# Attention and two feed-forward stages on one core: key scores in eight small matmuls, gate-weight splits ahead of the activation's, a new operand order, an earlier load

## The chip, the cores and the metric

The kernel runs on one core of a Trainium2 chip. The metric is the device time of one execution in microseconds (us), from the first to the last instruction with what lies around it. All arithmetic is in 32-bit floats. On TensorE most operands are split into a high part (type fp32r) and a low part, and three matmuls (high by high, low by high, high by low) stand for one.

## The reference, cut to what matters

```
sm_attn(qq, kk, vv): softmax(qq kk^T / sqrt(64)) vv        # 8 batches, 8 heads, 576 positions, head size 64
p_packed = sm_attn(p, k, v)                                # p: 32 rows for each head
out = sm_attn(q, p_packed, p_packed)
x = rows of out, 4608 x 512
xn = x / rms(x) * rms_g
y = (silu(xn @ w_gate) * (xn @ w_val)) @ w_out             # 512 -> 1536 -> 512
h = y @ w_in ; g = max(h, 0) + alpha * min(h, 0)
result = g @ w_out2                                        # 512 -> 2048 -> 512
```

## The kernel before

The order of the instructions on every engine is the order in which the program issues them; a scheduler does not move them. Each engine works through its own list in order and waits at an instruction whose operands, or whose output buffer, are not ready.

The program has an opening, a first phase of 12 chunks (`CH`, `c` = 0 to 11) of 512 or 320 token columns, and a second phase over five pairs of token blocks for the last feed-forward stage. The change touches the opening and the first phase.

In the first phase a chunk runs over 12 steps (`f`, blocks of 128 of the 1536 hidden units). A step makes a gate tile and a value tile in PSUM (`blk_in`, the second tensors `ps_g`, `ps_v`), takes Tanh on ACT, multiplies on DVE, splits the result into `hh` (ACT) and `hl` (DVE) in `hsplit`, and one step later `blk_out` multiplies them by the output weights into four accumulators `ps_y`. The operands of `blk_in` are the normalized attention weights `xh`, `xl` of the chunk's tokens and, instead of values and gate weights apart, their product: `wg_job(b, j)` multiplies the packed values of batch `b` by the `j`-th part of the gate and value weights (`ps_wg`, L685) and splits it into `wgh` (ACT) and `wgl` (DVE). `JOBS` says in which steps these jobs run.

Between these matmuls stands the attention of later batches and chunks. `k_steps` (one for each batch) attends from `p` to the keys and values, `q_steps` from the queries to the packed result. Both are generators, and `work` and `burst` advance them a little at fixed places of a step: `burst` those pieces that give TensorE work, `work` the vector pieces. In `k_steps`, S1 transposes `p`, S2 transposes the keys of a group of four heads, S3 makes their scores, EX the exponentials, S4 transposes these and S5 multiplies by the values.

The tiles `ps_g`, `ps_v`, `ps_at` and `ps_wg` take turns in four PSUM banks (`bank`), so that a new gate tile must wait until one of the tiles before it has been read. `conv` (opening and chunk 0) and `late` (`conv_late`, from chunk 1) convert weights that arrive as 64-bit words; `next(late)` runs in odd steps at the third call of `work`, and in every step of a 512-column chunk.

All DMAs are issued by SP, in program order.

In the kernel before, `pbd` holds `p` with the rows of two heads on the diagonal of a 64-row tile and zeros beside them, and a key tile holds, for each partition, the same row of the four heads side by side. So the scores are full matmuls over two heads at once:

```
nc.tensor.transpose(t[...], kv_t[b, "k", g][:, r, 2 * c:2 * c + 2, :], ident[0:KP, 0:KP])
nc.tensor.matmul(out=t[c * 64:(c + 1) * 64, 0:w], lhsT=pT[:, 2 * g + c, :],
                 rhs=kT[g][:, c * S + hf * w:c * S + (hf + 1) * w], start=True, stop=True)
```

Of the kernel before, what the change touches and what calls it, by code (L numbers as in the profile page):

```python
# [8 lines left out]
F32 = mybir.dt.float32  # L9
# [9 lines left out]
def attention_moe_moe2_kernel(ctx, tc, q, k, v, p, w_gate, w_val, w_out, rms_g, w_in2, w_out2, alpha, out):  # L19
    nc = tc.nc  # L20
# [105 lines left out]
    with tc.manual_schedule():  # L126
# [18 lines left out]
        def load_p(b):  # L145
            for e in range(2):
                for g in range(G):
                    nc.sync.dma_start(
                        out=pbd[(e ^ g) * NP:(e ^ g) * NP + NP, 2 * g:2 * g + 2, e * D:(e + 1) * D],
                        in_=p[b].rearrange("(g c e) n d -> e g n c d", g=G, e=2)[e, g],  # L150
                    )
# [6 lines left out]
        def load_kv():  # L158
            if not kv_list:
                return  # L160
            if late_kv[0] is not None and kv_list[-1][0]:
                late_kv[0] += 1
                return
            b, nm, g = kv_list.pop()
            t = ap.tile([KP, HG * KR, D], F32, tag="kv", name=nm + "t", bufs=3)
            src = (k if nm == "k" else v)[b, g * HG:(g + 1) * HG].rearrange("h (p r) d -> p h r d", r=KR)
            if nm == "k":
                t = t.rearrange("p (r h) d -> p r h d", r=KR)
                for h in range(HG):
                    nc.sync.dma_start(out=t[:, :, h], in_=src[:, h])  # L170
            else:
                t = t.rearrange("p (h r) d -> p h r d", r=KR)
                nc.sync.dma_start(out=t, in_=src)
            kv_t[b, nm, g] = t
# [189 lines left out]
        def k_steps(b, bk):  # L364
            par = b % 2
            yield 2
            pT = ap.tile([128, H // 2, 64], F32, tag="pT", name="pT")
# [3 lines left out]
            def S1():  # L371
                t = bk()
                for c in range(4):
                    nc.tensor.transpose(t[:, c * 64:(c + 1) * 64], pbd[:, c, :], ident[0:64, 0:64])
                return lambda: evac(pT, t[:, 0:256].rearrange("p (c x) -> p c x", c=4), True)

            def S2(g, n):
                t = bk()
                if n == 0:
                    kT[g] = ap.tile([128, 2 * S], F32, tag="kT", name="kT")  # L380
                for m in range(4):
                    c, r = divmod(4 * n + m, KR)
                    nc.tensor.transpose(
                        t[:, m * KP:(m + 1) * KP], kv_t[b, "k", g][:, r, 2 * c:2 * c + 2, :], ident[0:KP, 0:KP]
                    )
                return lambda: evac(kT[g][:, n * 384:(n + 1) * 384], t[:, 0:384], n % 2 == 0 or b < 2)

            def S3(g):
                w = S // 2
                for hf in range(2):  # L390
                    t = bk()
                    for c in range(2):
                        nc.tensor.matmul(
                            out=t[c * 64:(c + 1) * 64, 0:w],
                            lhsT=pT[:, 2 * g + c, :],
                            rhs=kT[g][:, c * S + hf * w:c * S + (hf + 1) * w],
                            start=True, stop=True,
                        )
                    s1[g, hf] = t
# [9 lines left out]
            def EX(g):  # L409
                w = S // 2  # L410
                E1[g] = ap.tile([128, S], F32, tag="E1", name="E1")
                for hf in range(2):
                    nc.scalar.activation(
                        out=E1[g][:, hf * w:(hf + 1) * w], in_=s1.pop((g, hf))[:, 0:w], func=ACTF.Exp,
                        bias=st[g][:, 2:3], scale=scale, accum_out=st[g][:, 3 + hf:4 + hf],
                    )
# [332 lines left out]
        qa.run()  # L749
        conv(2)  # L750
        warmup(3)
        qb.run()
        conv(2)
        qb.run()
        warmup(3)
        conv(2)
        qa.run()
        conv(2)
        warmup(3)
        qa.run()  # L760
        qb.run(2)
        conv_to(4)
        wg_job(0, 0)
        xh, xl = new_x()
        for ids, o in of_chunk[0]:
            x_split(ids, xh, xl, o)
# [118 lines left out]
        for c, (t0, n, cuts) in enumerate(CH):  # L885
# [72 lines left out]
            def blk_in(f, off, tag):  # L958
                t = bank(tag)[:, 0:n]
                j, o = f // 2, off + f % 2 * 128  # L960
                for lo, hi, b in cuts:
                    for g in range(G):
                        wh, wl = wgt[b, j, g]
                        mm3(
                            t[:, lo:hi], wh[:, o:o + 128], wl[:, o:o + 128],
                            xh[:, g, lo:hi], xl[:, g, lo:hi], g == 0, g == G - 1,
                        )
# [8 lines left out]
            for f in range(NF):  # L976
# [33 lines left out]
                nc.vector.tensor_tensor(out=s, in0=s, in1=tv, op=ALU.mult)  # L1010
                hs[f] = hsplit(s, n)
# [263 lines left out]
```

## Time and profile before

| | |
|---|---|
| Median of 3 runs | 1677.42 us (1677.4 to 1677.53) |
| Profiled execution | 1677.25 us, span 1675.5 us |
| Mean granted TensorE clock | 0.989 |
| TensorE (PE) busy | 1605.1 us, 96% |
| VectorE (DVE) busy | 1124.2 us, 67% |
| ScalarE (ACT) busy | 708.8 us, 42% |
| GpSimd (POOL) busy | 278.7 us, 17% |

A share of busy time is a mean over stages with different limits. What counts for this change is where TensorE stands idle, what it then waits for, and how long the pieces take that are replaced. One fp32 matmul leaves two records, so that "x8" can be four matmuls.

### The profile page before, as it was taken

The numbers are of one execution on the slowest core, as the hardware profiler recorded it, in microseconds if no ns is written. First come the engines' busy times: TensorE is split into PE (matmuls) and PEld (weight loads), VectorE is DVE, ScalarE is ACT, GpSimd is POOL, SyncE is SP. The second block draws the span as 40 slices with busy tenths as digits, with TensorE's granted clock in tenths as the row PEclk, the third lists the DMA queues.
The fourth block names the chain that finished last, engine by engine and source line by source line (L and its number), as shares of the span: only waits on it lengthen the run. The fifth ranks groups of instructions, "written<-read, shape, count | busy, mean of one in ns | idle before, by whom it ended". The sixth has DMA issues, their size and how long they took to land.

```text
span 1675.5 us, 28072 instructions
## 1 busy us (share of the span) xinstructions
PE 1605.1 (96%) x10378; PEld 1341.9 (80%) x10378; DVE 1124.2 (67%) x2109; ACT 708.8 (42%) x1533; POOL 278.7 (17%) x262
## 2 busy tenths in 40 slices
PE   6799899999999999999999999999999999999998
PEld 4466787888878878888888788888888888987997
DVE  4786557666566665665547888677757775776775
ACT  3566445555455454555445333421341133224224
POOL 1442123233233311001002662000000000000000
PEclk9699999999999999999999999999999999999999
DMA  9876546635565465663334665734464455657553
GB/s 223 274 238 190 171 125 184 174 83 178 161 187 165 131 208 169 209 195 117 115 101 156 232 232 193 266 138 170 157 232 150 158 174 203 217 198 264 189 183 126
DMA packets 234472, 303.07 MB, mean 181 GB/s; under 512 B 95200, under 2 KB 113632, under 8 KB 234336
## 3 DMA queue, kind: packets, MB, share of 16 engines
q1 hardware_dynamic: 234336, 301.28, 56.0%
q8 instruction: 82, 1.34, 0.3%
q14 instruction: 54, 0.44, 0.1%
HBM read 245.64 MB, written 55.57 MB: 180 GB/s over the span
## 4 chain that ended last, share of the span: by engine, by line
PE 44%; DVE 5%; DMA 2%; ACT 2%; issue 2%; POOL 1%; SPq 0%; DVEq 0%; ACTq 0%; POOLq 0%
PE ps_g L122 7%; PE ps_g L123 7%; PE ps_g L124 7%; PE ps_y L123 7%; PE ps_y L122 7%; PE ps_y L124 7%; DVE hl L113 1%; DMA in_l<-os_dram 1%; DVE in_l L113 1%; POOL i_raw L863 1%; ACT hh L110 1%; DMA i_raw<-w_dram 1%; DMA in_l<-lo_dram 1%; DVE tl L1073 1%; PE ps_v L123 1%
## 5 line engine op out<-in xcount | busy, mean ns | idle before, releaser
L122 PE MATMUL ps_y<-hh,in_h 128*128 128x320 f32 (+1 forms) x576 | 207.1, 360 | 3.5 <-ACT hh L110 3.5
L110 ACT ACTIVATE hh<-tl 128x512 fp32r<-128x512 f32 (+1 forms) x80 | 47.1, 588 | 375.2 <-DVE tl L1080 375.2
L124 PE MATMUL ps_y<-hh,in_l 128*128 128x320 f32 (+1 forms) x576 | 195.2, 339 | 2.6 <-DMA in_l<-lo_dram 2.6
L123 PE MATMUL ps_y<-hl,in_h 128*128 128x320 f32 (+1 forms) x576 | 195.6, 340 | 0.6
L1006 DVE SCALAR_TENSOR_TENSOR s<-s,ps_g 128x320 f32<-128x320 f32 (+1 forms) x132 | 71.3, 540 | 143.2 <-ACT s L1001 143.0
L110 ACT ACTIVATE hh<-s 128x320 fp32r<-128x320 f32 (+1 forms) x144 | 75.6, 525 | 213.3 <-DVE s L1010 213.3
L122 PEld LDWEIGHTS ps_y<-hh,in_h 128*128 128x128 f32 x576 | 109.1, 189 | 56.5 <-issue 43.0
L113 DVE TENSOR_TENSOR hl<-s,hh 128x320 fp32r<-128x320 f32 (+1 forms) x144 | 85.2, 592 | 85.1 <-ACT hh L110 85.1
L122 PE MATMUL ps_g<-xh,wgh 128*128 128x256 f32 (+3 forms) x384 | 123.3, 321 | 12.7 <-DVE wgl L113 4.9
L320 POOL TENSOR_TENSOR in_l<-w_raw,in_h 128x512 fp32r<-128x512 f32 x72 | 93.8, 1302 | 216.6 <-ACT in_h L110 176.0
L122 PE MATMUL ps_g<-yh,w 128*128 128x512 f32 (+1 forms) x336 | 125.3, 373 | 3.9 <-ACT th L1181 3.8
L123 PE MATMUL ps_g<-yl,w 128*128 128x512 f32 (+1 forms) x336 | 124.8, 371 | 0.0
L124 PE MATMUL ps_g<-yh,w 128*128 128x512 f32 (+1 forms) x336 | 124.8, 371 | 0.0
L123 PE MATMUL ps_g<-xl,wgh 128*128 128x256 f32 (+3 forms) x384 | 117.0, 305 | 4.5 <-DVE xl L113 4.5
L124 PEld LDWEIGHTS ps_y<-hh,in_l 128*128 128x128 f32 x576 | 109.1, 189 | 11.7 <-DMA in_l<-lo_dram 3.4
L122 PE MATMUL ps_v<-xh,wgh 128*128 128x256 f32 (+3 forms) x384 | 116.8, 304 | 0.2
L124 PE MATMUL ps_g<-xh,wgl 128*128 128x256 f32 (+3 forms) x384 | 116.3, 303 | 0.0
L123 PEld LDWEIGHTS ps_y<-hl,in_h 128*128 128x128 f32 x576 | 109.5, 190 | 8.3 <-DVE hl L113 1.9
L123 PE MATMUL ps_v<-xl,wgh 128*128 128x256 f32 (+3 forms) x384 | 116.1, 302 | 0.0
L124 PE MATMUL ps_v<-xh,wgl 128*128 128x256 f32 (+3 forms) x384 | 115.9, 302 | 0.0
L122 PE MATMUL ps_y<-in_h,hh 128*128 128x512 f32 x288 | 112.4, 390 | 1.6 <-DMA in_h<-os_dram 0.9
L123 PE MATMUL ps_y<-in_l,hh 128*128 128x512 f32 x288 | 113.2, 393 | 0.7 <-DVE in_l L113 0.2
(184 smaller groups left out, 4002.8 us busy)
## 6 DMA issues: line engine op xcount, KB each, us to landing
w<-w_dram SPq DMA_DIRECT2D x224, 256.0 KB, 5.1
gv_raw<-gv_dram SPq DMA_DIRECT2D x168, 256.0 KB, 3.7
o_raw<-w_dram SPq DMA_DIRECT2D x52, 512.0 KB, 4.1
w_dram<-w SPq DMA_DIRECT2D x88, 256.0 KB, 2.2
in_l<-lo_dram SPq DMA_DIRECT2D x59, 256.0 KB, 4.2
w<-in_moe_w_out_dram SPq DMA_DIRECT2D x28, 512.0 KB, 4.0
kt<-in_k_dram SPq DMA_DIRECT2D x64, 144.0 KB, 3.5
vt<-in_v_dram SPq DMA_DIRECT2D x16, 576.0 KB, 5.5
```

Source lines behind the costliest of these rows:

```text
L110: nc.scalar.activation(out=hi, in_=src, func=ACTF.Copy)
L113: nc.vector.tensor_tensor(out=lo, in0=src, in1=hi.bitcast(F32), op=ALU.subtract)
L122: nc.tensor.matmul(out=o, lhsT=lh, rhs=rh, start=first, stop=False, skip_group_check=more)
L123: nc.tensor.matmul(out=o, lhsT=lh, rhs=rl, start=False, stop=False, skip_group_check=more)
L124: nc.tensor.matmul(out=o, lhsT=ll, rhs=rh, start=False, stop=last, skip_group_check=more)
L320: nc.gpsimd.tensor_tensor(out=l, in0=raw[u], in1=h.bitcast(F32), op=ALU.subtract)
L863: nc.gpsimd.tensor_tensor(out=out, in0=x, in1=y, op=op)
L1006: nc.vector.scalar_tensor_tensor(out=s, in0=s, scalar=1.0, in1=tg, op0=ALU.add, op1=ALU.mult)
L1073: nc.vector.tensor_tensor(out=out, in0=x, in1=y, op=ALU.add)
```

## The change

It has five parts.

1. **Keys by row pairs.** `p` is loaded twice, once into each half of the head dimension's 128 columns (`pd`, two DMAs in place of four, and no zeros to write first). A key tile now lies head by head in the order of DRAM, so that a group is loaded in one DMA (two for batch 0) in place of four, in runs of 1,536 bytes in place of 256. S2 transposes two neighbouring rows of one head at a time: even rows land on partitions 0 to 63, odd rows on 64 to 127. S3 makes the scores in eight matmuls of 64 rows by 32 columns, each at its own place in the array (`tile_position`), even rows into one bank and odd rows into the other. EX writes the two banks interleaved.
2. **Combined gate weights split ahead of the activation.** From chunk 1 on the job of a step is issued right after the product, ahead of `hsplit` and of the second call of `work`, and no longer in `burst`.
3. **The operand's low part last in a chunk's first tile.** In step 0 of each chunk the six matmuls of a cut take `xh` four times and then `xl` twice.
4. **Late weights loaded a step ahead.** The first `next(late)` only issues loads.
5. **A new order of the opening**, in which the two query chains and the conversions alternate in smaller pieces, and each `x_split` follows its own chain.

```
-        pbd = ap.tile([64, H // 2, 128], F32, name="pbd")
+        pd = ap.tile([128, G, 2, D], F32, name="pd")
...
-        nc.vector.memset(pbd, 0.0)
...
+            src = p[b].rearrange("(g h) n d -> (h n) g d", g=G)
             for e in range(2):
...
+                nc.sync.dma_start(out=pd[:, :, e, :], in_=src)
...
-            if nm == "k":
-                t = t.rearrange("p (r h) d -> p r h d", r=KR)
-                for h in range(HG):
-                    nc.sync.dma_start(out=t[:, :, h], in_=src[:, h])
...
+            t = t.rearrange("p (h r) d -> p h r d", r=KR)
+            n_h = 2 if nm == "k" and b == 0 else HG
+            for h in range(0, HG, n_h):
+                nc.sync.dma_start(out=t[:, h:h + n_h], in_=src[:, h:h + n_h])
...
         def conv_late():
             ahead = [load_wide(u, one, NST) for u in units2[:2]]
+            yield
...
+                for e in range(2):
+                    s1[g, e] = bk()
+                for h in range(HG):
+                    for e in range(2):
+                        rows = slice(e * D, (e + 1) * D)
                         nc.tensor.matmul(
...
+                            out=s1[g, e][(h ^ g) * NP:(h ^ g) * NP + NP, 0:w],
+                            lhsT=pT[rows, g, h * NP:(h + 1) * NP],
+                            rhs=kT[g][rows, h * w:(h + 1) * w],
                             start=True, stop=True,
+                            tile_position=(e * D, (h ^ g) * NP),
                         )
...
-                for jb in jobs:
+                for jb in jobs if c == 0 else ():
                     wg_job(*jb)
...
+                for lo, hi, b in cuts if f == 0 else []:
+                    steps = [(xh, w, g) for w in range(2) for g in range(G)]
+                    steps += [(xl, 0, g) for g in range(G)]
...
                 nc.vector.tensor_tensor(out=s, in0=s, in1=tv, op=ALU.mult)
+                for jb in JOBS[c].get(f, ()) if c else ():
+                    wg_job(*jb)
                 hs[f] = hsplit(s, n)
                 work(f, 2)
```

On TensorE the order outside the opening and outside step 0 of a chunk stays; what stands in it changes. In step 1 of chunk 0, after a gate-weight job, the scores of a key group (`kT`, `pT`) stood ahead of `blk_out` like this before:

```order
L685 MATMUL ps_wg<-gv_raw,ppG 32x512 x8
L393 MATMUL ps_at<-kT,pT 64x288 x4
L122 MATMUL ps_y_567<-hh,in_h 128x512
L123 MATMUL ps_y_567<-hl,in_h 128x512
L124 MATMUL ps_y_567<-hh,in_l 128x512
```

and stand like this now:

```order
L683 MATMUL ps_wg<-gv_raw,ppG 32x512 x8
L390 MATMUL ps_at<-kT,pT 32x288 x8
L122 MATMUL ps_y_558<-hh,in_h 128x512
L123 MATMUL ps_y_558<-hl,in_h 128x512
L124 MATMUL ps_y_558<-hh,in_l 128x512
```

Four matmuls that give 64 rows of scores have become eight that give 32, at the same place. There are 16 such groups in the program, two of them in the opening and three in chunk 0.

On DVE, in steps 1 and 2 of chunk 1, the first late conversion (its weights are `w_1896`, its result `w_1900`) stood right behind the splits of step 1, and the query chain's transposes out of PSUM (`A_1925<-ps_at`) behind it:

```order
L1006 SCALAR_TENSOR_TENSOR s<-s,ps_g 128x320
L1010 TENSOR_TENSOR s<-s,ps_v 128x320
L113 TENSOR_TENSOR hl<-s,hh 128x320
L113 TENSOR_TENSOR wgl<-ps_wg,wgh 128x512 x2
L232 TENSOR_SCALAR w_1900<-w_1896 128x512
L578 STREAM_TRANSPOSE A_1925<-ps_at 128x256 x2
L580 TENSOR_REDUCE s_1770<-A_1925 128x16
```

Now the same steps read:

```order
L1023 SCALAR_TENSOR_TENSOR s<-s,ps_g 128x320
L1027 TENSOR_TENSOR s<-s,ps_v 128x320
L113 TENSOR_TENSOR wgl<-ps_wg,wgh 128x512 x2
L113 TENSOR_TENSOR hl<-s,hh 128x320
L576 STREAM_TRANSPOSE A_1908<-ps_at 128x256 x2
L578 TENSOR_REDUCE s_1756<-A_1908 128x16
```

The conversion has left the place ahead of the transposes (it now stands two steps later), and `wgl` stands ahead of `hl`.

In step 3 of chunk 2 DVE had a query chain's transpose (`A2T`) and `hl` ahead of `wgl`:

```order
L1010 TENSOR_TENSOR s<-s,ps_v 128x320
L113 TENSOR_TENSOR hl<-s,hh 128x320
L597 STREAM_TRANSPOSE A2T<-A_2957 128x512
L113 TENSOR_TENSOR wgl<-ps_wg,wgh 128x512 x2
L238 SCALAR_TENSOR_TENSOR w_2932<-w_2462,w_2932 128x512
```

and has now:

```order
L1027 TENSOR_TENSOR s<-s,ps_v 128x320
L113 TENSOR_TENSOR wgl<-ps_wg,wgh 128x512 x2
L113 TENSOR_TENSOR hl<-s,hh 128x320
L595 STREAM_TRANSPOSE A2T<-A_2938 128x512
L225 TENSOR_SCALAR w_3054<-w_2606 128x512
```

The two instructions that stood between the product and `wgl` now come after it, and the late conversion is one piece further back in its own sequence.

## Rows read from the trace of the kernel before

**Rows 1.** Page, busy us (share of the span) xinstructions.

```profile
PE 1605.1 (96%) x10378; PEld 1341.9 (80%) x10378; DVE 1124.2 (67%) x2109; ACT 708.8 (42%) x1533; POOL 278.7 (17%) x262
```

**Rows 2.** Waits of PE: waiter <- waited for: us in total, times, longest.

```profile
PE ps_g L122 <- DVE wgl L113: 4.9, 5, 1.4
PE ps_g L123 <- DVE xl L113: 4.5, 7, 1.0
PE ps_at L550 <- DVE A L578: 3.5, 1, 3.5
...
PE ps_at L608 <- DVE A2T L597: 2.8, 3, 2.1
...
PE ps_y L383 <- DMA kt<-in_k_dram: 1.3, 2, 0.8
```

**Rows 3.** Timeline of PE, 504 to 507 us: start, duration, line, operation [idle before].

```profile
504.67 0.31 PE L123 MATMUL ps_y<-hl,in_h 128*128 128x320 f32 x1
504.81 0.31 PE L124 MATMUL ps_y<-hh,in_l 128*128 128x320 f32 x1
505.05 1.19 PE L393 MATMUL ps_at<-kT,pT 128*64 128x288 f32 x8
506.17 0.41 PE L122 MATMUL ps_g<-xh,wgh 128*128 128x320 f32 x1
```

**Rows 4.** Timeline of PE, 176 to 178 us.

```profile
176.31 0.31 PE L124 MATMUL ps_y<-hh,in_l 128*128 128x320 f32 x1
176.55 0.66 PE L567 MATMUL ps_at<-qT,ppB 64*32 64x256 f32 x16
177.15 0.30 PE L122 MATMUL ps_g<-xh,wgh 128*128 128x64 f32 x1
```

**Rows 5.** Timeline, 172 to 188 us (chunk 1): SP, DVE and PE.

```profile
176.53 0.38 SPq L219 DMA_DIRECT2D w<-in_moe_w_in_dram  x1
...
182.80 0.43 DVE L232 TENSOR_SCALAR w<-w 128x512 int32<-128x512 int32 x1 [6.14 <-DMA w<-in_moe_w_in_dram]
...
183.64 0.60 PE L550 MATMUL ps_at<-ident,qt 64*128 64x64 f32 x4 [3.47 <-DVE A L578]
...
184.17 0.63 PE L122 MATMUL ps_y<-hh,in_h 128*128 128x320 f32 x1
...
187.24 0.31 PE L124 MATMUL ps_y<-hh,in_l 128*128 128x320 f32 x1
```

**Rows 6.** Windows: stretch, length, busy us of each engine, granted clock, DMA share, GB/s.

```profile
185.00:190.00 5.00, 5.00 (x31) 4.18 (x30) 3.41 (x10) 2.65 (x4) 0.34 (x1) 0.78 0.24 52
```

**Rows 7.** Timeline, 263 to 269 us (chunk 2): PE and DVE.

```profile
263.48 1.09 PE L685 MATMUL ps_wg<-gv_raw,ppG 64*32 64x512 f32 x16
...
266.48 0.49 DVE L113 TENSOR_TENSOR hl<-s,hh 128x320 fp32r<-128x320 f32 x1 [0.54 <-ACT hh L110]
...
267.52 1.25 DVE L113 TENSOR_TENSOR wgl<-ps_wg,wgh 128x512 fp32r<-128x512 f32 x2
268.22 0.42 PE L122 MATMUL ps_g<-xh,wgh 128*128 128x320 f32 x1 [1.42 <-DVE wgl L113]
```

**Rows 8.** Timeline of PE, two waits, in chunk 0 and chunk 3.

```profile
94.54 0.50 PE L122 MATMUL ps_g<-xh,wgh 128*128 128x512 f32 x1 [0.23 <-DVE wgl L113]
...
315.34 0.41 PE L123 MATMUL ps_g<-xl,wgh 128*128 128x320 f32 x1 [1.05 <-DVE xl L113]
```

**Rows 9.** Timeline, 1 to 10 us (the opening): SP and PE.

```profile
1.42 1.80 SPq L148 DMA_DIRECT2D pbd<-in_p_dram  x4
3.26 5.41 SPq L170 DMA_DIRECT2D kt<-in_k_dram  x8
...
8.98 0.36 PE L383 MATMUL ps_y<-ident,kt 96*128 96x96 f32 x2 [0.77 <-DMA kt<-in_k_dram]
```

**Rows 10.** Page, DMA issues: xcount, KB each, median us from issue to landing.

```profile
kt<-in_k_dram SPq DMA_DIRECT2D x64, 144.0 KB, 3.5
vt<-in_v_dram SPq DMA_DIRECT2D x16, 576.0 KB, 5.5
```

**Rows 11.** Timeline, 47 to 52 us (end of the opening): PE.

```profile
47.45 1.96 PE L685 MATMUL ps_wg<-gv_raw,ppG 64*32 64x512 f32 x16
...
51.65 0.80 PE L122 MATMUL ps_g<-xh,wgh 128*128 128x512 f32 x1 [2.24 <-ACT xh L110]
```

More of the change, by code (lines that the diff above doesn't have):

```diff
@@ L145, in load_p @@
         def load_p(b):
+            src = p[b].rearrange("(g h) n d -> (h n) g d", g=G)
             for e in range(2):
[L147 to L151, printed above, removed]
+                nc.sync.dma_start(out=pd[:, :, e, :], in_=src)
         kv_list = [(b, nm, g) for b in range(B) for nm in "kv" for g in range(G)]
@@ L366, in k_steps @@
             yield 2
-            pT = ap.tile([128, H // 2, 64], F32, tag="pT", name="pT")
+            pT = ap.tile([128, G, 128], F32, tag="pT", name="pT")
             s1, kT, E1, E1T = {}, {}, {}, {}
@@ L372, in S1 @@
                 t = bk()
-                for c in range(4):
-                    nc.tensor.transpose(t[:, c * 64:(c + 1) * 64], pbd[:, c, :], ident[0:64, 0:64])
-                return lambda: evac(pT, t[:, 0:256].rearrange("p (c x) -> p c x", c=4), True)
+                for g in range(G):
+                    nc.tensor.transpose(t[:, g * 128:(g + 1) * 128], pd[:, g].rearrange("p e d -> p (e d)"), ident)
+                return lambda: evac(pT, t[:, 0:256].rearrange("p (g x) -> p g x", g=G), True)
             def S2(g, n):
@@ L381, in S2 @@
                 for m in range(4):
-                    c, r = divmod(4 * n + m, KR)
+                    h, r = divmod(4 * n + m, KR // 2)
                     nc.tensor.transpose(
-                        t[:, m * KP:(m + 1) * KP], kv_t[b, "k", g][:, r, 2 * c:2 * c + 2, :], ident[0:KP, 0:KP]
+                        t[:, m * KP:(m + 1) * KP],
+                        kv_t[b, "k", g][:, h, 2 * r:2 * r + 2, :].rearrange("p r d -> p (r d)"), ident[0:KP, 0:KP],
                     )
@@ L413, in EX @@
                     nc.scalar.activation(
-                        out=E1[g][:, hf * w:(hf + 1) * w], in_=s1.pop((g, hf))[:, 0:w], func=ACTF.Exp,
+                        out=E1[g].rearrange("p (r e x) -> p e r x", e=2, x=KP)[:, hf],
+                        in_=s1.pop((g, hf))[:, 0:w].rearrange("p (r x) -> p r x", x=KP), func=ACTF.Exp,
                         bias=st[g][:, 2:3], scale=scale, accum_out=st[g][:, 3 + hf:4 + hf],
@@ L748, in attention_moe_moe2_kernel, with some @@
         qb = Chain(q_steps((2, 3), bk_pro), 0)
-        qa.run()
+        def some(ch, n):
+            for _ in range(n):
+                ch.next()
+        xh, xl = new_x()
+        (ids_a, o_a), (ids_b, o_b) = of_chunk[0]
+        some(qa, 6)
+        qb.run()
         conv(2)
         warmup(3)
[L752 to L757, printed above, removed]
+        some(qa, 3)
+        some(qb, 6)
         conv(2)
         warmup(3)
-        qa.run()
-        qb.run(2)
+        some(qa, 4)
+        some(qb, 3)
+        conv(2)
+        warmup(3)
+        some(qa, 3)
+        x_split(ids_a, xh, xl, o_a)
+        some(qb, 4)
+        conv(2)
         conv_to(4)
         wg_job(0, 0)
-        xh, xl = new_x()
-        for ids, o in of_chunk[0]:
-            x_split(ids, xh, xl, o)
+        some(qb, 3)
+        x_split(ids_b, xh, xl, o_b)
+        assert qa.kind is None and qb.kind is None
         conv_to(5)
@@ L960, in blk_in @@
                 j, o = f // 2, off + f % 2 * 128
-                for lo, hi, b in cuts:
+                os_ = slice(o, o + 128)
+                for lo, hi, b in [] if f == 0 else cuts:
                     for g in range(G):
@@ L964, in blk_in @@
                         mm3(
-                            t[:, lo:hi], wh[:, o:o + 128], wl[:, o:o + 128],
+                            t[:, lo:hi], wh[:, os_], wl[:, os_],
                             xh[:, g, lo:hi], xl[:, g, lo:hi], g == 0, g == G - 1,
+                        )
+                for lo, hi, b in cuts if f == 0 else []:
+                    steps = [(xh, w, g) for w in range(2) for g in range(G)]
+                    steps += [(xl, 0, g) for g in range(G)]
+                    for n_, (x, w, g) in enumerate(steps):
+                        nc.tensor.matmul(
+                            out=t[:, lo:hi], lhsT=wgt[b, j, g][w][:, os_], rhs=x[:, g, lo:hi],
+                            start=n_ == 0, stop=n_ == len(steps) - 1,
                         )
```

10 lines of the change are left out of this document (removed).

## The prediction

> **What bounds the kernel now.** I read the page first. TensorE is busy 96% of the span [rows 1], so the span is TensorE's own work and about 70 us in which it stands idle. A change helps if it takes away work of TensorE or one of these idle pieces; a faster vector engine alone gives nothing. The second view was the list of PE's waits [rows 2], which says who ended the idle pieces. The reader sees that none is large: 4.9 us for `wgl`, 4.5 us for `xl`, 3.5 us behind one DVE transpose, 2.8 us for `A2T`, 1.3 us for the first keys. Then I went with the timeline to the place of each, to see what the waiting instruction really hangs on, and to the score matmuls, to see what one group costs.
>
> **The change part by part.** I count each part in TensorE's time. Where TensorE is dense, a matmul of 320 columns starts 0.14 to 0.15 us after the one before, as the first two of [rows 3] do; I write 0.147.
>
> *Scores in eight small matmuls.* The last dense matmul ahead of a score group starts at 504.81, the first behind it at 506.17 [rows 3]. Without the group the second would start 0.147 later, so the group costs 1.36 - 0.147 = 1.21 us. The new form is not in the trace, but its nearest kin is: the query scores L567, eight matmuls of 64 rows by 32 columns at eight places of the array, on 256 columns. They cost 177.15 - 176.31 - 0.147 = 0.69 us [rows 4]. The new form has 288 columns; if the 0.60 us from the group's start to the next matmul grew in that ratio, it would be 0.68, so the cost is at most 0.69 + 0.08 = 0.77, and if only the part that streams grows, less; I take 0.74. A group saves 1.21 - 0.74 = 0.47 us. There are 16: two in the opening, on the chain that everything waits for, three in chunk 0, where DVE often holds TensorE up and I count half, and eleven later. That is 14.5 x 0.47 = **6.8 us**. The bounds are nothing, if even and odd rows do not overlap, and 16 x 0.55 = 9 us. The transposes S1 and S2 move the same number of columns as before, and EX the same number of elements; I count them at nothing, hidden behind TensorE's own stream.
>
> The Trainium skill ("TensorE: Matmul & The Clock Gate", Measured speedup vs the span model) gives for such packed matmuls one matmul's duration plus about 4 ns for each further one. L393's four, which share the array in pairs, take 505.05 to 506.17, so one alone would be about 0.56; by the rule eight would then cost 0.59, an estimate, and the term would be 14.5 x 0.62 = 9.0 us instead. The row of L567 has the lead-in and the change of shape in it, and I stay with it.
>
> *The opening.* Two waits of TensorE for the first keys sum to 1.3 us [rows 2], the second of them 0.77 us at 8.98 [rows 9]. SP spends 1.80 us to issue four DMAs of `p`, and 5.41 us for eight of keys, which start at 3.26 [rows 9]. With two and four, and no zeros to wait for, SP is done some 3.6 us earlier. I count both waits as gone: **1.3 us**, between nothing (the larger pieces land later) and 3.6. The end of the opening I count at nothing. There TensorE waits 2.24 us for ACT's `xh` at 51.65 [rows 11]. In the new order the second query chain gets through TensorE earlier, but the gate weights' conversion on POOL then stands ahead of L685, and behind L685 come `wgl`, the chain's last multiplication and its `x_split` in a row; what is won ahead of 47.45 goes there. I bound it by 1.5 us either way, less than that wait.
>
> *Late weights.* In chunk 1 SP issues the first late load at 176.53, and DVE, which has the conversion next in its list, stands until it lands at 182.80, 6.14 us idle [rows 5]. Queued behind it are the transposes that empty the query scores' banks, and TensorE waits 3.47 us for one of these. The granted clock of the stretch behind is 0.78 [rows 6], a mixture of 2.4 and 1.2 GHz: the twelve matmuls from 184.17 to 187.24 take 3.07 us for eleven steps, where dense ones take 11 x 0.147 = 1.62. Wait and slow clock are 3.47 + 1.45 = **4.9 us**. The load is still issued there, but DVE comes to the conversion two steps later. A step has at least 24 matmuls of 0.147 us, 3.5 us, and attention pieces, so that is 7 us or more, when data that needed 6.3 us (176.53 to 182.80) are there. If that cover is gone, the same wait comes back in step 3.
>
> *Gate weights ahead of the activation.* L685 is done at 264.57; `hl` starts only at 266.48 and `wgl` at 267.52, with the query chain's transpose between them [rows 7]. TensorE wants a bank for the next gate tile from 266.80 and gets one at 268.22, 1.42 us later. Ahead of `hl`, `wgl` can start at 265.94 (where DVE's 0.54 us idle before `hl` begins), if ACT's copies, which now come ahead of `hh` and need only L685, are done by then, and the first bank is free at about 266.6. So this wait goes. Of the five of this kind [rows 2] only the 0.23 us at 94.54 lies in chunk 0 [rows 8], where the job stays put: 4.9 - 0.2 = **4.7 us**. What now stands behind `wgl` (1.25 us) and the two copies on ACT is `hh`, `hl` and the chain's vector pieces. `hh` and `hl` are used only a step later. The chain's pieces are not so far ahead.
>
> *Operand order.* `xl` is asked for by the second matmul of a chunk, from now on by the fifth: three matmuls later, 0.44 us at 320 columns and 0.35 at 256. Six of the seven waits are longer than that (the longest 1.05 us [rows 8]), four at 320 columns and two at 256, and one is 0.2 us in chunk 0: 4 x 0.44 + 2 x 0.35 + 0.2 = **2.7 us** of 4.5.
>
> *Given back.* DVE delivers chain pieces up to 1.25 us later in the steps with a job. TensorE already waits 2.8 us for `A2T` [rows 2]. I add half as much again: **-1.5 us**; bounds 0 and 6.
>
> The sum is 6.8 + 1.3 + 4.9 + 4.7 + 2.7 - 1.5 = 18.9 us. The profiled execution took 1677.25 us, 0.17 under the median, so I forecast **1658.5 us**.
>
> **The rivals.** *The small matmuls do not overlap* (slower). If each of the eight took as long as one of today's four, 1.12/4 = 0.28 us, a group would cost 2.24 + 0.1, 1.13 more than now, and the 16 groups would add 18 us instead of saving 6.8: 1658.5 + 25 = about 1683 us. It decides from about 2.0 us a group, where the other 12 us are used up. For it: even and odd rows write the same partitions, of two banks. Against it: L567 uses the same eight places. 4%.
>
> *The waits move on* (DVE is late with something else). If `wgl` and `xl` give back all that they take, 7.4 us: 1666 us. For it: DVE has 67%, and the waits for `A2T` show that it is late with chain pieces in places. Against it: most of the freed time lies at steps whose next DVE results are not wanted for several us. 14%.
>
> *The late load is still awaited*, in step 3, or SP comes to other loads later since the late stores fall into other steps: 4.9 us lost, 1663.5 us. 7%.
>
> *The opening gains more.* The key loads move 144 KB in 3.5 us, the value loads 576 KB in 5.5 [rows 10]; new key loads look like the value loads. If opening and chunk 0, in which TensorE often runs at the slower clock, start 3.6 us earlier and lose 4 us less to waits, the time is 1652 us. The Trainium skill ("DMA: Bandwidth & Descriptors", Specifications) asks for pieces of 512 bytes or more to run at line rate, which the old key loads with 256 bytes break and the new ones keep; the two rows agree with it. 16%.
>
> *No change that can be measured*, because the parts do not do what they say or chunk 0 loses what the rest wins: within 3 us of 1677. 5%. Another 4% lies beyond, slower, by a conversion order in chunk 0 that keeps DVE late there.
>
> **How the numbers follow.** The forecast has 50%. Its own range, from the bounds of the score term (0 to 9), the opening (-1.5 to 5) and what is given back (0 to 6), is 1653 to 1665. With the larger opening below and the moved waits above it the range is 1648 to 1669; outside it are the two slower cases, no change, and a few per cent below. Under 0.2% (3.4 us) a measurement of this kernel can hardly tell a difference from none. Slower: the 4% of the first rival and half of the last 4%, 6%. Within the bound: 5% and the other half, 7%. Faster: 87%.
>
> **What would show it.** Right: the score groups L390 take about 0.66 us from first record to the next matmul; PE has no wait for `wgl` over 0.5 us after chunk 0 and waits about 2 us for `xl` in total; no idle near 180 us, and a clock of 1.00 there; the first score group about 1 us earlier. The second phase, from about 925 us before, should come earlier as a whole by the gain and keep its own length. Wrong: score groups of 1.2 us or more, new waits for `A2T`, `hl` or an exponential in steps with jobs, a DVE wait for late weights in step 3, or an opening whose first gate tile is not earlier than 51.65 us.

## The result and the profile after

The changed kernel takes 1661.01 us (median of 4 executions, 1658.24 to 1662.17), the kernel before 1677.47 us beside it: a ratio of 0.9897, with a 95% interval of 0.988 to 0.9914. A second measurement of both gave 1660.43 and 1678.32 us, 0.9895 (0.9881 to 0.991). So the change is worth 16.5 to 17.9 us, where 18.9 were forecast.

The profiled execution took 1660.02 us with a span of 1658.2, 17.3 less than before. The page's first part:

```profile
PE 1598.2 (96%) x10490; PEld 1339.9 (81%) x10490; DVE 1121.8 (68%) x2108; ACT 711.0 (43%) x1533; POOL 273.3 (16%) x262
```

Set against [rows 1], TensorE's work fell by 6.9 us and its idle time from 70.4 to 60.0 us, by 10.4. The share stays at 96%: the number that tells is the idle time, not the share. Who ends it now, from PE's waits (in total, times, longest):

```profile
PE ps_at L390 <- DVE s L1027: 5.3, 2, 4.5
PE ps_wg L683 <- POOL gv_raw L234: 4.8, 3, 3.1
PE ps_y L124 <- DMA in_l<-lo_dram: 4.1, 3, 1.4
...
PE ps_at L606 <- DVE A2T L595: 2.3, 2, 2.1
PE ps_y L438 <- DMA vt<-in_v_dram: 2.1, 1, 2.1
...
PE ps_y L123 <- DVE hl L113: 1.7, 5, 0.3
...
PE ps_y L606 <- DVE A2T L595: 1.4, 1, 1.4
...
PE ps_at L606 <- DVE A L576: 1.3, 2, 0.8
...
PE ps_g L122 <- DVE wgl L113: 0.2, 1, 0.2
```

Of [rows 2], `wgl` is down to the 0.2 us of chunk 0, and `xl`, the transpose `A` ahead of the query scores and the first keys are gone. New are five waits for `hl`, each about 0.3 us, and two for the query chain's `A` ahead of L606, one step behind a gate-weight job. In the opening a wait of 2.1 us for the values (`vt`) and one of 1.4 us for `A2T` are new. The wait for the weights' low parts (`in_l`) was 2.6 us before and is 4.1 now.

A score group in a dense stretch of chunk 5 (timeline of PE):

```profile
491.50 0.31 PE L124 MATMUL ps_y<-hh,in_l 128*128 128x320 f32 x1
491.74 0.71 PE L390 MATMUL ps_at<-kT,pT 64*32 64x288 f32 x16
492.38 0.41 PE L122 MATMUL ps_g<-xh,wgh 128*128 128x320 f32 x1
```

From dense matmul to dense matmul it is 0.88 us, less 0.147: a group costs 0.73 us where it cost 1.21 [rows 3]. That the eight run side by side is seen in the opening, where the records are apart (eight more follow from 8.27):

```profile
8.00 0.43 PE L390 MATMUL ps_at<-kT,pT 64*32 64x288 f32 x1
8.01 0.43 PE L390 MATMUL ps_y<-kT,pT 64*32 64x288 f32 x1
...
8.05 0.43 PE L390 MATMUL ps_y<-kT,pT 64*32 64x288 f32 x1
```

All eight start within 0.05 us, and each lasts 0.43. The granted clock is 1.00 there.

In chunk 1 the late load is still issued at the same point of the program. The timeline of SP, PE and DVE there, and under it the windows (busy us of each engine, granted clock, DMA share, GB/s):

```profile
175.41 0.38 SPq L212 DMA_DIRECT2D w<-in_moe_w_in_dram  x1
...
178.99 0.46 PE L548 MATMUL ps_at<-ident,qt 64*128 64x64 f32 x4
...
189.44 1.20 DVE L225 TENSOR_SCALAR w<-w 128x512 int32<-128x512 int32 x1
```
```profile
180.00:185.00 5.00, 5.00 (x54) 4.21 (x56) 3.69 (x9) 3.02 (x7) 0.00 (x0) 1.00 0.48 148
185.00:190.00 5.00, 5.00 (x57) 3.57 (x57) 3.68 (x7) 3.83 (x9) 2.23 (x2) 1.00 0.58 164
```

DVE comes to the conversion 14 us after the load's issue and does not wait; the transposes at 178.99 follow the matmul before them, where there were 3.47 us of idle time [rows 5] and a clock of 0.78 [rows 6].

The step of chunk 2 that [rows 7] showed:

```profile
255.04 1.09 PE L683 MATMUL ps_wg<-gv_raw,ppG 64*32 64x512 f32 x16
...
257.54 1.28 DVE L113 TENSOR_TENSOR wgl<-ps_wg,wgh 128x512 fp32r<-128x512 f32 x2
...
258.29 0.41 PE L122 MATMUL ps_g<-xh,wgh 128*128 128x320 f32 x1
...
258.74 0.48 DVE L113 TENSOR_TENSOR hl<-s,hh 128x320 fp32r<-128x320 f32 x1
```

`wgl` starts 2.5 us after the job's first matmul, not 4.0, and the gate tile starts without a wait. `hl` now comes 1.2 us after `wgl`'s start.

The opening, timeline of SP and PE, and two rows on DMA issues (xcount, KB each, median us to landing):

```profile
0.74 0.94 SPq L147 DMA_DIRECT2D pd<-in_p_dram  x2
...
1.73 1.94 SPq L166 DMA_DIRECT2D kt<-in_k_dram  x4
...
44.23 3.15 PE L683 MATMUL ps_wg<-gv_raw,ppG 64*32 64x512 f32 x8 [3.14 <-POOL gv_raw L234]
...
50.06 1.22 PE L981 MATMUL ps_g<-xh,wgh 128*128 128x512 f32 x2 [2.06 <-ACT xh L110]
```
```profile
vt<-in_v_dram SPq DMA_DIRECT2D x16, 576.0 KB, 5.5
kt<-in_k_dram SPq DMA_DIRECT2D x14, 576.0 KB, 6.1
```

SP has the first keys issued at 3.7 us instead of 8.7 [rows 9], and the first scores start at 8.00. The first gate tile comes 1.6 us earlier than in [rows 11]: half of the 3.2 us won at the head (the first scores started at 11.20) is lost before it, and just ahead of it TensorE stands 3.14 us for POOL's conversion of the gate weights. These are single executions. In the eight profiled ones with this opening (this one and experiments 2, 3, 4, 7, 8, 9 and 11) the first gate tile starts at 48.3 to 50.9 us, so the lead over the one profile before is 0.7 to 3.4 us.

**Where the 17.3 us lie.** I followed the activation of each gate tile through both traces (after less before, by its start on ACT): -1.9 us at chunk 0's first step, -1.1 at its last; -6.1 in step 2 of chunk 1, where the late load's wait stood; -8.4 at chunk 2, -11.6 at chunk 4, -13.7 at chunk 6. From the end of chunk 7 to the start of chunk 8 it goes back, from -14.3 to -12.7, and it is -15.7 at the end of chunk 11. The last 1.6 us fall in the second phase, where the difference goes to and fro by up to 1.1 us at a step.

### The profile page after: what moved, and what is told of

The parts are those of the page before. It is cut to its first block, busy times and chain, and to the rows that moved or that the text cites. A ratio compares the mean times of both kernels' runs of the same rounds, so it can differ in the third digit from the quotient of the medians.

```text
span 1658.2 us, 28225 instructions
## 1 busy us (share of the span) xinstructions
PE 1598.2 (96%) x10490; PEld 1339.9 (81%) x10490; DVE 1121.8 (68%) x2108; ACT 711.0 (43%) x1533; POOL 273.3 (16%) x262
## 4 chain that ended last, share of the span: by engine, by line
PE 78%; DVE 10%; ACT 4%; DMA 3%; issue 2%; SPq 2%; POOL 1%; DVEq 0%; ACTq 0%; POOLq 0%
PE ps_y L122 11%; PE ps_y L123 11%; PE ps_y L124 11%; PE ps_g L122 10%; PE ps_g L123 10%; PE ps_g L124 10%; PE ps_wg L683 3%; PE ps_v L122 2%; PE ps_v L123 2%; PE ps_v L124 2%; DVE hl L113 1%; ACT hh L110 1%; DVE s L1027 1%; DMA w<-in_moe_w_gate_dram 1%; DVE s L1023 1%
## 5 line engine op out<-in xcount | busy, mean ns | idle before, releaser
L124 PEld LDWEIGHTS ps_y<-hh,in_l 128*128 128x128 f32 x576 | 109.8, 191 | 13.7 <-DMA in_l<-lo_dram 5.3
L122 PE MATMUL ps_g<-xh,wgh 128*128 128x256 f32 (+3 forms) x352 | 113.0, 321 | 6.5 <-ACT pT L117 2.3
L123 PE MATMUL ps_g<-in_l,hh 128*128 128x512 f32 x288 | 112.8, 392 | 0.3 <-DVE in_l L113 0.2
L124 PE MATMUL ps_y<-in_h,hl 128*128 128x512 f32 x288 | 112.4, 390 | 0.0
L122 PE MATMUL ps_g<-in_h,hh 128*128 128x512 f32 x288 | 112.2, 389 | 0.3 <-ACT in_h L110 0.3
L124 PE MATMUL ps_g<-in_h,hl 128*128 128x512 f32 x288 | 112.4, 390 | 0.0
L110 ACT ACTIVATE in_h<-w_raw 128x512 fp32r<-128x512 f32 x144 | 90.3, 627 | 41.4 <-PE ps_y L123 38.7
```

The lines of the kernel that those rows point to most:

```text
L110: nc.scalar.activation(out=hi, in_=src, func=ACTF.Copy)
L122: nc.tensor.matmul(out=o, lhsT=lh, rhs=rh, start=first, stop=False, skip_group_check=more)
L123: nc.tensor.matmul(out=o, lhsT=lh, rhs=rl, start=False, stop=False, skip_group_check=more)
L124: nc.tensor.matmul(out=o, lhsT=ll, rhs=rh, start=False, stop=last, skip_group_check=more)
```

## The experiments

The first five undo one part each. Medians vary between measurements of one kernel, those of the kernel before from 1677.47 to 1679.09 us. So a part is also read from the profiled trace: how much later the activations come than in the changed kernel, after what the first step of chunk 1 differs by is taken off where the part doesn't touch what lies ahead of it. Experiment 11 shows how far such a reading can be trusted.

**1. Old scores** (part 1 undone: `p` and key loads, S1 to S3, EX).

```
-                            out=s1[g, e][(h ^ g) * NP:(h ^ g) * NP + NP, 0:w],
-                            lhsT=pT[rows, g, h * NP:(h + 1) * NP],
...
+                            out=t[c * 64:(c + 1) * 64, 0:w],
+                            lhsT=pT[:, 2 * g + c, :],
```

> The changed kernel with its first part undone (keys side by side, four score matmuls for a group, zeros in the tile of p); all else as changed. Theory of the sum: the score groups cost 1.21 us again and the first keys are waited for again, 6.8 + 1.3 = 8.1 us more than the changed kernel's 1661.0, 1669 us; nearly all of it outside chunk 0. Rival, the group's gain is hidden behind DVE in chunk 0 and gives back more elsewhere: 3 to 5 us more, 1665 us.

Measured: 1668.47 us (1665.16 to 1668.88), 7.5 over the changed kernel; 0.9937 (0.9923 to 0.9951) against before. In the trace the activations come 1.38 us later at chunk 0's start and 1.64 at its end. What its three groups are worth can't be read from these 0.26 us: over the same chunk the changed kernel's second execution loses 0.7 us against its first (experiment 11). From there it is 5.3 us to chunk 10 over eleven groups, 0.48 each, 7.0 in all. The wait for the first keys is back (2.2 us).

**2. Old late load** (part 4 undone).

```
             ahead = [load_wide(u, one, NST) for u in units2[:2]]
-            yield
```

> The changed kernel with only the late weights' first load again in the same step as its conversion. Theory of the sum: DVE stands about 6 us in step 1 of chunk 1, TensorE about 3.5 us and then runs slowly: 4.9 us more, 1666 us, all of it between the gate tiles of steps 1 and 2 of chunk 1. The step's shift also decides where SP is held by the late stores: if the three waits for low parts loaded back from DRAM (4.1 us in the changed kernel) come from the shift, they fall back to 2.6 us here and the net is 3.4 us, 1664.5 us. Rival, the wait is as long in another step: no difference.

Measured: 1668.4 us (1664.24 to 1672.65); 0.9943 (0.9927 to 0.9958). Timeline of it, chunk 1:

```profile
180.43 0.43 DVE L225 TENSOR_SCALAR w<-w 128x512 int32<-128x512 int32 x1 [6.25 <-DMA w<-in_moe_w_in_dram]
...
181.27 0.68 PE L547 MATMUL ps_at<-ident,qt 64*128 64x64 f32 x4 [3.98 <-DVE A L575]
```

Both waits are back (6.25 and 3.98 us, where the kernel before had 6.14 and 3.47), and the granted clock is 0.50 from 180 to 185 us. At this place the activations lose 5.5 us against the changed kernel. Between chunks 7 and 8 they win 1.7 back, since TensorE's waits for `in_l` sum to 1.2 us here and to 4.1 in the changed kernel; at the end of chunk 11 the loss is 5.5 us again. By medians it is 7.4 us, more than the 4.9 expected; the six times spread over 8 us, and the profiled one is the fastest.

**3. Old place of the gate-weight jobs** (part 2 undone).

```
-                for jb in jobs if c == 0 else ():
+                for jb in jobs:
...
-                for jb in JOBS[c].get(f, ()) if c else ():
-                    wg_job(*jb)
```

> The changed kernel with the gate-weight jobs again behind the activation's split. Theory of the sum: four waits for wgl of 0.7 to 1.4 us return, 4.7 us; the five waits of 0.34 us for hl at the ends of chunks, which the changed kernel has and the kernel before had not, go: 3.0 us more, 1664 us. Rival, the whole 4.7 us or more, because nothing was given back: 1666 us. Rival, none, because the waits for wgl came from the score groups' or the late loads' timing: 1661 us.

Measured: 1665.04 us (1662.67 to 1667.14); 0.9923 (0.9908 to 0.9939). PE's waits:

```profile
PE ps_g L122 <- DVE wgl L113: 5.0, 5, 1.6
...
PE ps_g L981 <- DVE xl L113: 1.1, 2, 0.6
```

`wgl` is back in full, `xl` in part, and the five waits for `hl` are gone. The trace loses 4.5 us by the end of chunk 11, the medians 4.0.

**4. Old operand order** (part 3 undone: step 0 like the other steps).

```
-                for lo, hi, b in [] if f == 0 else cuts:
+                for lo, hi, b in cuts:
...
-                for lo, hi, b in cuts if f == 0 else []:
-                    steps = [(xh, w, g) for w in range(2) for g in range(G)]
-                    steps += [(xl, 0, g) for g in range(G)]
```

> The changed kernel with the old order of operands in step 0 of a chunk. Theory of the sum: the waits for xl return, 2.7 to 4.5 us, 1663.7 to 1665.5 us, at the starts of chunks 2, 3, 4, 6, 7 and 9. Rival: the waits for xl went because the split of the activation now stands elsewhere in DVE's list, and the operand order does nothing: within 0.5 us of 1661.

Measured: 1660.61 us (1659.99 to 1663.22); 0.9899 (0.9884 to 0.9914), no difference from the changed kernel that the medians show. The trace has four waits for `xl`, 1.0 us in total, and loses 1.6 us by the end of chunk 7, at the starts of chunks, and 1.4 by the end of chunk 11.

**5. Old opening** (part 5 undone).

```
-        some(qa, 6)
-        qb.run()
+        qa.run()
...
-        some(qa, 4)
-        some(qb, 3)
+        qa.run()
```

> The changed kernel with the old order of the opening (the two query chains and the conversions in the old large pieces, the operands' splits together); all else as changed. Theory of the sum: the new order neither wins nor loses, since what the second query chain gains stands behind the conversion on POOL: 1661 us within 1 us, first gate tile within 1 us of the changed kernel's 50.06. Rival, the new order is what brings the opening forward: 1.5 us or more later. Rival, it costs: 1.5 us or more earlier, first gate tile before 48.6.

Measured: 1660.85 us (1659.05 to 1663.77); 0.9891 (0.9874 to 0.9909). The medians show no difference. PE in the profile:

```profile
37.73 0.69 PE L642 MATMUL ps_at<-ident,s 128*128 128x128 f32 x2 [5.56 <-DVE gv_raw L231]
...
48.36 1.22 PE L972 MATMUL ps_g<-xh,wgh 128*128 128x512 f32 x2 [2.24 <-ACT xh L110]
```

The first gate tile comes 1.7 us earlier than in the changed kernel's first profile, not within 1 us of it, and so at the mark that was set for the rival by which the new order costs. But the changed opening itself gave 48.3 to 50.9 us, so one profile doesn't decide. At chunk 1 0.9 us of the lead is left, at the end of chunk 11 nothing; 1.1 us go in step 5 of chunk 3, where the granted clock fell in this execution and not in the changed kernel's (last section). That the new order wins anything is not shown.

**6 and 12. Conversion ahead.** In the opening the gate weights' conversion goes ahead of the second query chain's four pieces in front of L683. It aims at the 3.14 us for POOL.

```
         x_split(ids_a, xh, xl, o_a)
-        some(qb, 4)
         conv(2)
+        some(qb, 4)
         conv_to(4)
         wg_job(0, 0)
```

> The changed kernel with one conversion step of the opening moved ahead of the second query chain's last vector pieces, so that POOL can add the gate weights before it waits for that chain. Theory: the second half of the first gate-weight job waits for POOL (3.1 us idle at 44.23 and a job of 3.15 us in the changed kernel), and everything up to the first gate tile hangs on it: first gate tile about 2 us earlier, 1.5 to 2 us less in all, 1659 us. Rival, chunk 0 is held by DVE's backlog in step 1 and gives it back: 1661 us.

> The gate weights' conversion ahead of the second query chain's last pieces, once more beside the changed kernel. Theory: TensorE's wait for the converted weights at the end of the opening, 3.1 us in the changed kernel, is 1.0 to 1.5 us here, the first gate tile comes 3 to 4 us earlier, and 1 to 2 us of that are left at the end: 1658 to 1660 us, 1 to 2 us under the changed kernel of the same call. Rival: the earlier gate tile is an accident of the profiled executions: no difference over 0.5 us between the two medians.

Measured: 1660.17 us (1656.83 to 1660.26) and 1658.59 us (1657.5 to 1660.96), the ratios 0.988 (0.9862 to 0.9898) and 0.9884 (0.9867 to 0.99); that is 0.8 us under the changed kernel's first median and 1.8 under its second. Timeline of PE in the second one:

```profile
40.75 1.05 PE L683 MATMUL ps_wg<-gv_raw,ppG 64*32 64x512 f32 x4 [0.95 <-POOL gv_raw L234]
...
45.73 0.74 PE L981 MATMUL ps_g<-xh,wgh 128*128 128x512 f32 x2 [2.31 <-ACT xh L110]
```

The first gate tile comes 4.3 us earlier (3.8 in the first of the two profiles). Against all eight profiles of the changed opening it is at least 2 us earlier. 2.9 us are left at chunk 1 (3.1), and 1.6 at the end of chunk 11 (1.4); 1.1 us of what is lost go in step 5 of chunk 3, where the granted clock fell in both. It is the fastest version measured, by an amount at the edge of what can be told: the nine times have a mean of 1659.1 us, the eight of the changed kernel 1660.6, and both spread with a standard deviation of about 1.5 us.

**11. The changed kernel again.**

> The changed kernel itself once more, on the same chip as the next kernel, to learn how much of a difference of 1 us can be read between two versions. Theory: the opening and the start of the second phase vary from execution to execution by some us with the granted clock: 1659 to 1662 us, the single times spread over 3 to 4 us. Rival: the spread seen so far was that of a single profiled run: all times within 1 us.

Measured: 1660.43 us; the four times are 1662.46, 1661.27, 1659.58 and 1659.14. A difference of 1 us between medians is not to be read. The traces of the two executions differ as well: the second comes 0.55 us later to the first activation and 1.25 later to chunk 1; up to the end of chunk 7 this stays within 0.05 us, and at the end of chunk 11 it is 2.24. So what a part does between chunks 1 and 7 can be read to 0.1 us, but what it does to opening and chunk 0, or from chunk 8 on, only to about 1 us.

**7. The last step's job behind `hsplit`** (as before the change, in a chunk's last step only).

```
-                for jb in jobs if c == 0 else ():
+                for jb in jobs if c == 0 or f == NF - 1 else ():
...
-                for jb in JOBS[c].get(f, ()) if c else ():
+                for jb in JOBS[c].get(f, ()) if c and f < NF - 1 else ():
```

> The changed kernel, but in the last step of a chunk the gate-weight job stands behind the activation's split as before. Theory: the five waits of 0.34 us for hl at the ends of chunks (1.7 us) come from the jobs there and go, but xl is then late again at one or two starts of chunks (0.5 us each): 0.5 to 1.7 us less, 1660 us. Rival, they come from something else and stay: 1661 us.

Measured: 1662.05 us (1660.49 to 1663.4); 0.9895 (0.9878 to 0.9912). The waits for `hl` (1.7 us) are gone, and two for `xl` (1.1 us) are back; nothing is won by it. The trace is 1.3 us ahead at chunk 1 and 0.3 behind at the end of chunk 11; 1.1 of these 1.6 us go in step 5 of chunk 3, with the clock, as in experiment 5. The jobs of last steps thus carry both: `xl`, or `hl`, stands behind them.

**8. First late load in chunk 0's last step.**

```
+                    if at == 3 and f == NF - 1:
+                        next(late, None)
```

> The changed kernel, but the first late load is issued in the last step of chunk 0, so that the late conversions stand in the same steps as in the kernel before and their data are still there in time. Theory: the wait in chunk 1 stays away, and the waits for low parts loaded back (4.1 us) fall to the 1.2 us of the run with the old late load, since the late stores hold SP in other steps: 2.9 us less, 1658 us. Rival, these waits hang on other things than the shift: 1661 us.

Measured: 1660.83 us (1658.9 to 1663.36); 0.9889 (0.9871 to 0.9907). PE's waits between 655 and 860 us:

```profile
PE ps_y L124 <- DMA in_l<-lo_dram: 1.1, 3, 0.5
PE ps_g L122 <- DVE s L1025: 0.9, 1, 0.9
PE ps_y L123 <- DVE hl L113: 0.7, 2, 0.3
PE ps_at L606 <- DVE A2T L595: 0.5, 1, 0.5
```

The loads' waits fall by 3.0 us, but the three waits for DVE, 0.5 us together in the changed kernel, are 2.1 here, and the gain of 1.7 us at the start of chunk 8 is nearly gone by chunk 10.

**9. Jobs and order both old** (the edits of experiments 3 and 4 together).

> Parts 2 and 3 are undone together. Undone alone, part 2 cost about 4.5 us in the trace (and brought 1.1 us of waits for xl back), part 3 about 1.3 us (1.0 us of waits for xl). Theory: most of the 4.5 us that TensorE waited for xl came from the gate-weight splits standing in the way on DVE, so part 2 alone removes three quarters of it; with both undone all of it returns beside the 4.7 us for wgl: waits for xl of 4 to 4.5 us in total, and a time of 1668 to 1670 us, 7 to 9 us over the changed kernel. Rival: the two parts add up, as the prediction had them: waits for xl of about 2 us, and 1661 + 4.5 + 1.3 = 1666 to 1667 us.

Measured: 1670.23 us (1668.72 to 1671.63); 0.9947 (0.9935 to 0.996). PE's waits:

```profile
PE ps_y L124 <- DMA in_l<-lo_dram: 5.7, 4, 2.0
...
PE ps_g L122 <- DVE wgl L113: 4.7, 5, 1.5
...
PE ps_g L123 <- DVE xl L113: 2.9, 6, 0.9
```

The time is near the theory's, the waits are not: `xl` stands for 2.9 us, between the two. Up to the end of chunk 7 the trace loses 6.2 us, where the two parts alone lost 4.2 and 1.6, so there the rival is right and they add up. The further 3.5 us come behind that. The waits for `in_l` are 1.6 us longer than in the changed kernel, and behind two of them (1.77 us at 668.96, 2.02 us at 747.88) the granted clock falls. Windows (PE busy, granted clock, DMA share, GB/s):

```profile
670.00:673.00 3.00, 3.00 (x9) 0.50 0.38 142
748.50:751.50 3.00, 3.00 (x13) 0.50 0.01 2
```

The changed kernel's first profile has 1.00 in both places; its second falls in the latter too, and loses 0.7 us there. So part of the 3.5 us is the clock's. All five times lie above 1668.7, so each execution lost more than the two parts' sum; whether for this reason, one trace can't show.

**10. Early late load and conversion ahead** (the edits of experiments 8 and 6 together).

> Two edits together, each of which alone came out within 1 us of the changed kernel: the first late load is issued in the last step of chunk 0 (which took the waits for the weights' low parts from 4.1 to 1.1 us, but had given its gain back by chunk 10), and in the opening the gate weights' conversion stands ahead of the second query chain's last pieces. Theory: the time behind chunk 8 is set by DVE, so the waits that go there come back as others, and the opening's order is worth at most 1 us: 1659 to 1661 us. Rival: the gains add up and stay: 1657 to 1658 us.

Measured: 1659.4 us (1658.72 to 1660.23); 0.9882 (0.9867 to 0.9897). 1.0 us under the changed kernel's second median, and 0.8 under one and 0.8 over the other of the two medians of the conversion alone: that the gains add up is not shown.

## Why the prediction held

The forecast was 1658.5 us, the range 1648 to 1669; the time is 1661.01. Term by term:

| term | forecast | found |
|---|---|---|
| scores and first keys | 6.8 + 1.3 = 8.1 | 7.0 in the trace, 5.3 of it behind chunk 0; 7.5 by medians |
| late weights | 4.9 | 5.5 in the trace, 7.4 by medians |
| gate-weight jobs | 4.7 | 4.8 of waits, 4.5 net; 4.0 by medians |
| operand order | 2.7 | 1.4 alone; none by medians |
| new opening order | 0 | none by medians |
| given back | 1.5 | 1.7 at `hl`, 1.3 at `A` |

The range is wide. The bounds given for the terms, added up, would be 1651 to 1673 us; the "own range" of 1653 to 1665 is narrower than that without a reason given.

*Scores.* The cost of the new form was read off its nearest kin, L567, as 0.74 us and is 0.73. The saving of 0.48 us a group held in the eleven groups behind chunk 0 (5.3 us). What chunk 0 gave of the 0.7 us counted for it can't be read. It did give part back, as expected: there TensorE comes earlier and waits longer. One score group now waits 4.47 us for DVE's product, at 70.69 us, where it waited 3.85 before and in experiment 1:

```profile
70.69 1.21 PE L390 MATMUL ps_at<-kT,pT 64*32 64x288 f32 x14 [4.47 <-DVE s L1027]
```

The Trainium skill ("TensorE: Matmul & The Clock Gate", Measured speedup vs the span model) had the further matmuls start about 4 ns after one another. The trace has 0.05 us for seven steps, 7 ns, near it; the price worked out from it, 0.59 us a group, was too low by 0.14, and the row of the kin was the better guide.

*Late weights.* The wait and the slow clock behind it went as described, and experiment 2 brought both back. The rival that had SP come later to other loads was partly right: the waits for `in_l` grew by 1.5 us, and they shrink with the load elsewhere. They are 1.1 to 1.3 us in the three profiles where the first late load stands elsewhere (experiments 2, 8 and 10) and 3.8 to 5.7 in the ten where it stands in its new place. Their place was not step 3 of chunk 1 but chunks 7 to 9, and the price 1.5 us against the kernel before, 3 against the same kernel with the load elsewhere, where 4.9 had been allowed. Taken away they come back as waits for DVE (experiment 8). That the late stores holding SP are the reason was expected, and no run shows it.

*Gate weights and `xl`.* Here a term was mis-sized, and its mechanism was incomplete. Both waits were counted as separate causes. With the jobs moved, TensorE waits 1.0 us for `xl` in the old operand order (experiment 4), where it waited 4.5 [rows 2]; with the jobs back too, 2.9 (experiment 9), and with the jobs alone back 1.1 (experiment 3). So the jobs' move alone takes 1.9 us of the 4.5, because the split of a chunk's last job stood ahead of `xl` on DVE (experiment 7 shows it for two of them), another 1.6 went with the parts 1, 4 and 5 without my having traced to which, and the operand order has 1.0 left to remove. It does remove all of that. Alone it would have taken 1.8 of the 2.9; the two share 0.8.

*Given back.* The waits found are twice what was counted, and the place was wrong. `A2T`, on which the 1.5 us were based, stands for 3.7 us where it stood for 2.8, but 1.4 of that are at 37.15 us in the opening; in the chunks it fell to 2.3, and its longest wait, 2.1 us, stayed as it was. What comes late behind the moved jobs is `A`, another of the chain's pieces: two waits, 1.3 us, which the two profiles with the old jobs (3 and 9) don't have, and of which 0.2 is left where the first late load stands elsewhere (2, 8 and 10). The larger part is at `hl`, which the prediction called safe because it is used a step later. In a chunk's last step there is no later step: the last `blk_out` stands in the same one, and there `hl` is 0.3 us late.

*The opening.* The two waits for keys went (in other executions up to 1.0 us of them is left, experiment 9) and the first scores came 3.2 us earlier, but the first gate tile in this profile only 1.6: the conversion on POOL ahead of L683 took the rest, as forecast. The prediction's list of TensorE's waits left out the longest of all, in the opening, and gave it no term:

```profile
41.01 0.69 PE L644 MATMUL ps_at<-ident,s 128*128 128x128 f32 x2 [5.69 <-DVE gv_raw L238]
```

So "none is large: 4.9 us" was misread. With the new order this wait is gone, and those of 3.14 us for POOL and 1.41 for `A2T` stand in its place; with the old order it is back (5.56 us, experiment 5) and these two are gone. That one is exchanged for the others fits the count of nothing for the end of the opening, and it is luck, since the wait was not considered. The rival with 3.6 us at the opening did not come true in this kernel; moving the conversion ahead takes part of it (experiments 6 and 12).

*The sum.* Counted from chunk 1 on, to leave the scatter of the opening out, the parts undone one by one lose 5.3 + 5.5 + 4.5 + 1.4 = 16.7 us in the traces, and together they win 14.6. Two executions of the changed kernel differ by 1.0 us over the same stretch, so about half of the 2.1 us between may be scatter; the rest I have not followed. By medians the five parts lose 7.5 + 7.4 + 4.0 - 0.4 - 0.2 = 18.3 us, against 16.5 to 17.9 together. The second phase is no term: in the fourteen profiled executions it took 756.4 to 760.6 us from the last activation of chunk 11, so the 1.6 us by which it is shorter after than before may be scatter as well. Its scatter of 4 us is larger than the terms for the operand order and for what is given back. That the total came out within 2.5 us of the forecast is partly luck: the late weights gave more than their term, the operand order less, and twice as much was given back.

## What to carry to other kernels

Price a new form of a matmul by the nearest kin in the same trace, from dense matmul to dense matmul; lead-in and change of shape are then in the price. Two waits that end at instructions of one in-order engine are not two terms: ask what stood in that engine's list ahead of each, and count a common cause once. When one load is moved, look for the loads that now come late elsewhere: the late load's new place won 5.5 us at once and brought 3 us of waits for other loads. And run the unchanged kernel twice before a part is read from a trace: here two traces of it agree to 0.05 us over seven chunks and differ by 2.2 us at the end of the phase.

## What was unexpected of the hardware

The granted clock differs between executions with the same instructions at the same place. At the start of the second phase TensorE waits 2.2 to 2.9 us for ACT's Tanh in each of the fourteen profiled executions. Timeline of PE and, behind that matmul, windows (PE busy, granted clock, DMA share, GB/s), first of experiment 11:

```profile
923.07 0.50 PE L122 MATMUL ps_g<-yh,w 128*128 128x512 f32 x1 [2.83 <-ACT th L1200]
```
```profile
923.00:927.00 4.00, 3.93 (x17) 1.00 0.88 282
```

and the same of experiment 10:

```profile
918.54 0.80 PE L122 MATMUL ps_g<-yh,w 128*128 128x512 f32 x1 [2.83 <-ACT th L1202]
```
```profile
918.50:922.50 4.00, 3.96 (x9) 0.50 0.90 266
922.50:927.50 5.00, 5.00 (x19) 0.79 0.58 222
```

After the same wait, and dense work at the full clock ahead of it, the one goes on at 2.4 GHz and the other at 1.2, so that nine matmuls fit where the first has 17. The clock fell like this in six of the fourteen executions. The length of the wait does not tell which: it is 2.61 to 2.88 us in the six, 2.23 to 2.88 in the other eight. Against the changed kernel's first profile the fall costs 1.3 to 2.8 us over the next thirty matmuls, and 0.3 to 1.8 are left of it after a hundred, since a wait of 0.7 us that this profile has there is then gone. Experiment 10 was 3.7 us ahead of that profile at the end of chunk 11 and 2.2 at this wait, and is 0.3 us ahead at the end of the span.

It also falls where TensorE has waited less. In step 4 of chunk 3 TensorE waits 0.69 us twice, in the changed kernel's first profile (330.63 and 332.62) as in experiment 12 (327.72 and 329.71). Windows behind the second wait (PE busy, granted clock, DMA share, GB/s), first of the changed kernel:

```profile
333.00:336.00 3.00, 3.00 (x28) 1.00 0.00 0
```

and of experiment 12:

```profile
330.00:333.00 3.00, 3.00 (x12) 0.50 0.00 0
```

The clock fell there in four executions (experiments 5, 6, 7 and 12), and each took 1.1 us longer for the step than the changed kernel. What decides it is not shown.
